# Rounding keys and queries in one pass, with the score factor in the minimum: an attention and mixing kernel on one core

## The chip, the cores and the metric

The kernel runs on one core of one Trainium2 chip. The metric is device time in microseconds (us) of one execution; the kernel before took 984.07 us (median of 3 runs, 982.93 to 987.56). The engines are named as the profile names them: PE is TensorE's matmul, PEld its weight load, DVE is VectorE, ACT is ScalarE, POOL is GpSimd, SP is SyncE, which here only issues transfers.

## What is computed

Three stages follow each other: a causal attention with a decay, a Fourier mixing with a feed-forward block, and a second mixing with weights of its own. The change touches the attention alone (4 batches of 8 heads, 576 positions, 64 columns a head):

```python
scores = scale * np.matmul(q, k.transpose(0, 1, 3, 2))     # scale = 1/8
cum = np.cumsum(np.log(np.clip(f, 0.0001, 1.0)), axis=-1)
decay = cum[:, :, :, None] - cum[:, :, None, :]
scores = np.where(causal, -1000000000.0, scores + decay)
scores = scores - np.max(scores, axis=-1, keepdims=True)
attn = np.exp(scores)
attn = attn / (np.sum(attn, axis=-1, keepdims=True) + 1e-09)
out = np.matmul(attn, v)
```

## The kernel before

`phase1` walks over 32 heads, in 16 pairs. The matmuls of the scores take a rounded type, so each of q and k is cut into a rounded upper part and a lower part (value minus upper part), and the products upper times upper, lower times upper and upper times lower are summed. The rows of one head's operands are laid out for two matmuls:

- `hi` (128 x 2 x 576): plane 1 is the query, plane 0 the key. Both stand twice in `raw`, in rows 0 to 63 and again in rows 64 to 127. Rows 64 to 127 of plane 1 are overwritten with the query's lower part. L232 multiplies plane 1 by plane 0.
- `q2` (66 x 576, one buffer for even heads and one for odd ones): a second copy of the rounded query in rows 0 to 63 and ones in rows 64 and 65. `kl` (66 x 2 x 576, one for a pair): the key's lower part in rows 0 to 63, the running sum of the decay, in an upper and a lower part, in rows 64 and 65. L233 multiplies `q2` by `kl` into the same bank.

`prep_units` makes these for a head, from a `raw` of 128 x 2 x 576 that `load_head` (L191) brings from memory over SP's queue; there are two `raw` buffers, so the load for one head waits until the last reader of the head two before it is done. Per head: ScalarE rounds the query (L200); GpSimd takes the query's difference (L201); ScalarE rounds the key times -0.125 (L206; in every fourth head GpSimd does it, L204); GpSimd copies the query into `q2` (L210); VectorE takes the key's lower part (L211, again with the factor -0.125). For head 0 VectorE and ScalarE do all of it.

`score_units` then runs L232 and L233 for five blocks of query rows, into three rotating PSUM banks `pa`. VectorE empties each bank with one instruction that adds the mask, keeps the result in `P` and writes the row's minimum (L241; the scores are negated, so the minimum stands for the maximum). ScalarE takes exp of the minimum minus `P` (L246). After every second head VectorE turns the row sums into reciprocals (L248, L249) and GpSimd spreads them (L252). `turn_units` transposes `P` on TensorE (L271) and copies it out (L275 on ScalarE, L277 on VectorE); `av_units` multiplies by v (L306); `evac_pair` scales the outcome on VectorE (L322, L328), sends three rows through SP's queue (L331 to L338) and forms a sum and a difference on GpSimd (L341 `E`, L343 `O`). `fft_units` does the Fourier step of the batch before in between (L370 to L440: VectorE folds, ScalarE rounds, TensorE multiplies, `u` is formed on VectorE or GpSimd).

The loop pulls these generators in turn, a head's preparation one round ahead of its scores. What order the instructions stand in on each engine is then settled by a scheduler by priorities (scores 20, products with v 40) and by readiness as it reckons it; each engine runs its own list strictly in that order and waits at its head. From about 270 us on, the feed-forward and the last stage follow, which the change does not touch.

Of the kernel before, what the change touches and what calls it, by code (L numbers as in the profile page):

```python
# [13 lines left out]
ALU = mybir.AluOpType  # L14
# [41 lines left out]
class Net:  # L56
# [37 lines left out]
    def p1_open(self):  # L94
# [43 lines left out]
            nc.gpsimd.memset(z, 1.0)  # L138
        with tc.manual_schedule(engines={mybir.EngineType.DVE, mybir.EngineType.Activation}):
            nc.vector.memset(one, 1.0)  # L140
            nc.vector.memset(flag, 1.0)
            nc.vector.memset(flag[0:1], 0.0)
            fs, cs, hs = ([x[:, g * S : g * S + S] for g in range(2)] for x in (f0, c0, h0))
            for g in range(2):
                nc.vector.tensor_scalar(fs[g], fs[g], 1e-4, 1.0, ALU.max, ALU.min)
                nc.scalar.activation(fs[g], fs[g], AF.Ln)
            nc.vector.tensor_tensor_scan(cs[0], one[64:66], fs[0], 0.0, ALU.mult, ALU.add)
            nc.vector.tensor_scalar(lf, lf, 1e-4, 1.0, ALU.max, ALU.min)
            nc.vector.tensor_scalar(hs[0], cs[0], -1.0, None, ALU.mult)
            nc.vector.scalar_tensor_tensor(kl[64:66, 0], f(hs[0]), flag, cs[0], ALU.mult, ALU.add)  # L150
            for _ in self.prep_units(0, pair, raws[0], heads[0]):
                pass
            nc.scalar.activation(lf, lf, AF.Ln)
            nc.scalar.activation(self.rz[0][:, 0, 0:1], self.mask[:, 448:449], AF.Exp, scale=-1.0)


        def rest():
            nc.vector.tensor_tensor_scan(cs[1], one[64:66], fs[1], 0.0, ALU.mult, ALU.add)
            yield
            nc.vector.tensor_scalar(hs[1], cs[1], -1.0, None, ALU.mult)  # L160
            nc.vector.scalar_tensor_tensor(kl[64:66, 1], f(hs[1]), flag, cs[1], ALU.mult, ALU.add)
            yield from self.prep_units(1, pair, raws[1], heads[1])
            nc.vector.tensor_tensor_scan(cum, one[0:32], lf, 0.0, ALU.mult, ALU.add)
            nc.gpsimd.tensor_scalar(ch[:, 0], cum, 1.0, 1.0, ALU.mult, ALU.mult)
            nc.gpsimd.tensor_tensor(ch[:, 1], cum, f(ch[:, 0]), ALU.subtract)
            nc.gpsimd.dma_start(self.scr, ch)
            yield
# [26 lines left out]
    def prep_units(self, n, pair, raw, hd):  # L194
        nc = self.nc
        g = n % 2
        kl, q2 = pair["kl"], self.q2[g]
        hi = self.w2.tile([128, 2, S], F32R, tag="hi", name="hi")
        hd["hi"] = hi
        nc.scalar.copy(hi[:, 1], raw[:, 1])  # L200
        (nc.vector if n == 0 or n % 4 in [] else nc.gpsimd).tensor_tensor(hi[64:128, 1], raw[64:128, 1], f(hi[64:128, 1]), ALU.subtract)  # L201
        yield
        if n > 1 and n % 4 in [0]:
            nc.gpsimd.tensor_scalar(hi[:, 0], raw[:, 0], -0.125, 1.0, ALU.mult, ALU.mult)  # L204
        else:
            nc.scalar.activation(hi[:, 0], raw[:, 0], AF.Copy, scale=-0.125)  # L206
        if n == 0:
            nc.scalar.copy(q2[0:64], raw[0:64, 1])
        else:
            nc.gpsimd.tensor_scalar(q2[0:64], raw[0:64, 1], 1.0, 1.0, ALU.mult, ALU.mult)  # L210
        nc.vector.scalar_tensor_tensor(  # L211
            kl[0:64, g], raw[0:64, 0], -0.125, f(hi[0:64, 0]), ALU.mult, ALU.subtract
        )
        yield

    def score_units(self, hd, g):
        nc = self.nc
# [6 lines left out]
        for i in (4, 3, 2, 1, 0):  # L224
# [5 lines left out]
            with self.tc.high_priority(20):  # L230
                for t, a, b in parts:
                    nc.tensor.matmul(t[:, 0 : b - a], hi[:, 1, q], hi[:, 0, a:b], start=True, stop=False)  # L232
                    nc.tensor.matmul(t[:, 0 : b - a], q2[:, q], kl[:, g, a:b], start=False, stop=True)  # L233
                p = P[:, POFF[i] : POFF[i] + n0 + 128]
                lowest, least = mn[:, i : i + 1], 3.0e38
                for t, a, b in parts:
                    if b - a < n0 + 128 and a == 0:
                        to = mn[:, 5:6]
                    else:
                        to = lowest  # L240
                    nc.vector.tensor_tensor_reduce(  # L241
                        out=p[:, a:b], in0=t[:, 0 : b - a], in1=self.mask[:, S - n0 - 128 + a : S - n0 - 128 + b],
                        scale=1.0, scalar=least, op0=ALU.add, op1=ALU.min, accum_out=to,
                    )
                    least = to
                nc.scalar.activation(p, p, AF.Exp, bias=lowest, scale=-1.0, accum_out=zs[:, g, i : i + 1])  # L246
# [842 lines left out]
def constants():  # L1089
# [30 lines left out]
    alt = np.where(np.arange(258) % 2 == 0, 1.0, -1.0).astype(np.float32)[None, :]  # L1120
    alt[0, 257] = 0.0
    alt = np.concatenate([alt, np.zeros((127, 258), np.float32)])
    mask = np.where(np.arange(128)[None, :] <= np.arange(128)[:, None], 0.0, 1e30).astype(np.float32)
    return dict(dft=dft, alt=alt, mask=mask, ident=np.eye(128, dtype=np.float32))


# [53 lines left out]
```

## Time and profile before

| | |
|---|---|
| median of 3 runs | 984.07 us |
| lowest, highest | 982.93, 987.56 us |
| the profiled execution | 982.28 us |
| its span (first to last instruction) | 980.5 us |
| TensorE, share of the span | 94% |
| VectorE | 66% |
| ScalarE | 44% |
| GpSimd | 32% |

The shares are means over three stages. After about 300 us, in the feed-forward and the mixing, TensorE is busy nearly all the time and GpSimd for long stretches not at all; in the attention, the first 270 us, all four engines carry work. A row of the trace gives the start of an instruction in us from the span's start, its length in us, the engine and line, the tiles written and read with their shapes, and in brackets how long the engine had been idle before it and who released it. A TensorE that counts as busy includes the tail of a matmul in its pipeline, so it can be fed somewhat more densely than its busy share says.

### The profile page before, as it was taken

What the parts mean: (1) busy time and instruction counts of PE and PEld (TensorE: products, weight loads), DVE (VectorE), ACT (ScalarE), POOL (GpSimd) and SP (SyncE); (2) the same over time, 40 slices, a digit from 0 to 9 for tenths busy, and PEclk for the clock granted to TensorE, in tenths of its full rate; (3) what the DMA queues carried; (4) which work ended last, traced back from release to release, by engine and by line L of the source; (5) the groups of instructions that cost most, each with busy time, mean ns of one, the idle gap of its engine ahead of it and who ended that gap; (6) DMA issues with size and microseconds to landing.
All of it is one profiled execution on the core that took longest, in us unless ns stands there. A gap on an engine that the chain in (4) does not pass through costs nothing.

```text
span 980.5 us, 15893 instructions
## 1 busy us (share of the span) xinstructions
PE 917.6 (94%) x5960; PEld 852.3 (87%) x5960; DVE 644.3 (66%) x1503; ACT 427.8 (44%) x1038; POOL 312.9 (32%) x376
## 2 busy tenths in 40 slices
PE   4889898988978898999999999999999999999998
PEld 3667676766757798999999999999999999999998
DVE  7868778668678787625665366545677765746554
ACT  5887767667463243312332122112335543535331
POOL 5756356366433243300000000000014744525330
PEclk9999999999998799999999999999999999999999
DMA  4743322313032112001222222232420000000001
GB/s 144 205 124 112 100 87 79 111 63 94 21 96 68 53 44 87 1 1 43 87 87 88 85 87 87 86 132 92 140 70 1 1 14 37 2 37 14 25 26 49
DMA packets 24336, 68.04 MB, mean 69 GB/s; under 512 B 3534, under 2 KB 6990, under 8 KB 24260
## 3 DMA queue, kind: packets, MB, share of 16 engines
q1 hardware_dynamic: 20420, 62.52, 19.8%
q0 software_dynamic: 3120, 3.33, 1.4%
q10 hardware_dynamic: 720, 1.18, 0.4%
q8 instruction: 47, 0.77, 0.3%
q14 instruction: 29, 0.24, 0.1%
HBM read 57.92 MB, written 9.07 MB: 68 GB/s over the span
## 4 chain that ended last, share of the span: by engine, by line
PE 59%; DVE 12%; ACT 2%; issue 2%; POOL 1%; DMA 1%; SPq 0%; ACTq 0%; DVEq 0%; POOLq 0%
PE pa L738 18%; PE pb L752 11%; PE po L752 8%; PE pb L959 5%; PE pa L970 4%; PE pa L923 4%; PE po L959 3%; PE pt L306 1%; DVE kra L930 1%; DVE kra L947 1%; DVE kra L933 1%; DVE a L556 1%; DMA raw<-in_wf 1%; PE pb L399 1%; DVE kra L932 1%
## 5 line engine op out<-in xcount | busy, mean ns | idle before, releaser
L738 PE MATMUL pa<-un,wf 128*128 128x384 f32 x1152 | 220.1, 339 | 4.7 <-ACT wf L563 2.4
L738 PEld LDWEIGHTS pa<-un,wf 128*128 128x128 f32 x1152 | 202.7, 190 | 6.7 <-ACT wf L563 2.6
L744 DVE SCALAR_TENSOR_TENSOR h<-pa,h 128x384 fp32r<-128x384 f32 x96 | 53.2, 556 | 145.2 <-ACT h L743 145.2
L752 PE MATMUL pb<-h,wf 128*128 128x384 f32 x660 | 135.2, 337 | 0.3 <-DVE u L760 0.3
L246 ACT ACTIVATE P<-P,mn 128x512 f32<-128x512 f32 (+4 forms) x160 | 95.8, 601 | 60.3 <-DVE mn L241 59.8
L752 PEld LDWEIGHTS pb<-h,wf 128*128 128x128 f32 x660 | 116.9, 189 | 0.9 <-DVE u L760 0.6
L743 ACT ACTIVATE h<-pa 128x384 fp32r<-128x384 f32 x96 | 46.7, 489 | 148.7 <-PE pa L738 148.6
L752 PE MATMUL po<-h,wf 128*128 128x384 f32 x492 | 104.2, 340 | 2.9 <-DVE h L744 2.0
L959 PE MATMUL pb<-wtk,z 128*128 128x288 f32 x513 | 97.0, 294 | 0.0
L241 DVE CUSTOM_DVE_ANT_0 P<-pa,mask 128x512 f32<-128x512 f32 (+4 forms) x160 | 77.7, 508 | 28.7 <-PE pa L233 21.6
L915 POOL COPY xd<-u 128x64 f32<-128x64 f32 x32 | 6.8, 254 | 272.5 <-DVE u L760 264.3
L752 PEld LDWEIGHTS po<-h,wf 128*128 128x128 f32 x492 | 87.5, 190 | 4.3 <-DVE h L744 2.3
L271 PE MATMUL pb<-ident,P 128*128 128x128 f32 x480 | 83.8, 283 | 8.0 <-ACT PT L275 3.8
L232 PE MATMUL pa<-hi 128*128 128x448 f32 (+2 forms) x192 | 69.1, 383 | 20.4 <-DVE hi L201 11.1
L949 POOL TENSOR_TENSOR z<-kra,z 128x256 fp32r<-128x256 f32 x72 | 53.8, 766 | 86.9 <-ACT z L948 86.9
L959 PEld LDWEIGHTS pb<-wtk,z 128*128 128x128 f32 x513 | 79.2, 188 | 0.0
L959 PE MATMUL po<-wtk,z 128*128 128x288 f32 x351 | 75.1, 295 | 1.1 <-POOL z L949 1.1
L306 PE MATMUL pt<-PT,v 128*64 128x256 f32 (+4 forms) x448 | 66.6, 381 | 8.7 <-DVE X L322 3.6
L271 PEld LDWEIGHTS pb<-ident,P 128*128 128x128 f32 x480 | 56.7, 143 | 19.4 <-ACT PT L275 6.8
L233 PE MATMUL pa<-kl,q 66*128 66x448 f32 (+2 forms) x192 | 63.2, 363 | 1.4 <-DVE kl L211 1.4
L923 PE MATMUL pa<-wf,xs 128*128 128x256 f32 x456 | 63.9, 289 | 0.0
L232 PEld LDWEIGHTS pa<-hi 128*128 128x128 f32 x192 | 38.0, 202 | 29.7 <-ACT hi L206 11.0
(201 smaller groups left out, 1706.9 us busy)
## 6 DMA issues: line engine op xcount, KB each, us to landing
raw<-in_qk SPq DMA_DIRECT2D x31, 576.0 KB, 3.9
raw<-in_wf SPq DMA_DIRECT2D x32, 512.0 KB, 4.1
raw<-in_wtk SPq DMA_DIRECT2D x18, 288.0 KB, 2.8
v<-in_vp SPq DMA_DIRECT2D x16, 320.0 KB, 3.3
out<-ob SPq DMA_DIRECT2D x12, 288.0 KB, 2.1
dft<-in_dft POOLq DMA_DIRECT2D x8, 346.0 KB, 6.3
raw<-in_wth SPq DMA_DIRECT2D x4, 512.0 KB, 4.0
st_wth<-raw SPq DMA_DIRECT2D x4, 512.0 KB
```

The lines of the kernel that those rows point to most:

```text
L232: nc.tensor.matmul(t[:, 0 : b - a], hi[:, 1, q], hi[:, 0, a:b], start=True, stop=False)
L233: nc.tensor.matmul(t[:, 0 : b - a], q2[:, q], kl[:, g, a:b], start=False, stop=True)
L241: nc.vector.tensor_tensor_reduce(out=p[:, a:b], in0=t[:, 0 : b - a], in1=self.mask[:, S - n0 - 128 + a : S - n0 - 128 + b], scale=1.0, sca ...
L246: nc.scalar.activation(p, p, AF.Exp, bias=lowest, scale=-1.0, accum_out=zs[:, g, i : i + 1])
L271: nc.tensor.transpose(ps[:, o : o + 128], src, self.ident)
L306: nc.tensor.matmul(T[64 * g : 64 * g + 64, 256 + a : 256 + hi_q], v[:, j, g, :], hd["PT"][:, place[j, a] : place[j, a] + hi_q - a], start= ...
L738: nc.tensor.matmul(ps[:, 0:CH], t[:, l, 128 * d : 128 * d + 128], un[r][:, d], start=n == 0, stop=n == 11)
L744: nc.vector.scalar_tensor_tensor(h[:, 1], ps[:, 0:CH], 0.0, f(h[:, 0]), ALU.max, ALU.subtract)
L752: nc.tensor.matmul(outs[d], t[:, l, 128 * d : 128 * d + 128], h[:, r], start=k % G == 0 and n == 0, stop=k % G == G - 1 and n == 2,)
L923: nc.tensor.matmul(th, xs[:, l, d], self.wth[d][:, r, 256 * hf : 256 * hf + 256], start=n == 0, stop=n == 11)
L949: nc.gpsimd.tensor_tensor(z[:, 1], t, f(z[:, 0]), ALU.subtract)
L959: nc.tensor.matmul(acc[k][th], z[:, l, 128 * k : 128 * k + 128], self.wtk[kt][:, r, 288 * th : 288 * th + 288], start=first and i == 0 and ...
```

## The change

The factor 1/8 leaves the preparation. The instruction that empties the score banks (L241 before, L238 after) multiplies by -0.125 where it multiplied by 1; the mask is negated to fit, and the running sums of the decay are multiplied by -8, for heads 0 and 1 in the two instructions that make them anyway (L149, L150 and L160, L161), for all others by one more GpSimd instruction, once in the program (L164 after). Keys and queries need now only be rounded: one ScalarE copy of 128 x 1152 does both (L206 after). The two lower parts are two GpSimd differences in a row (L210 after). The copy of the rounded query into `q2` is a transfer on SP's queue from `hi` (L207 after). Head 0 keeps its own form: three ScalarE copies and two VectorE differences.

```diff
--- before.py
+++ after.py
@@ -138,7 +138,7 @@
             nc.gpsimd.memset(z, 1.0)
         with tc.manual_schedule(engines={mybir.EngineType.DVE, mybir.EngineType.Activation}):
             nc.vector.memset(one, 1.0)
-            nc.vector.memset(flag, 1.0)
+            nc.vector.memset(flag, 8.0)
             nc.vector.memset(flag[0:1], 0.0)
             fs, cs, hs = ([x[:, g * S : g * S + S] for g in range(2)] for x in (f0, c0, h0))
             for g in range(2):
@@ -146,21 +146,22 @@
                 nc.scalar.activation(fs[g], fs[g], AF.Ln)
             nc.vector.tensor_tensor_scan(cs[0], one[64:66], fs[0], 0.0, ALU.mult, ALU.add)
             nc.vector.tensor_scalar(lf, lf, 1e-4, 1.0, ALU.max, ALU.min)
-            nc.vector.tensor_scalar(hs[0], cs[0], -1.0, None, ALU.mult)
-            nc.vector.scalar_tensor_tensor(kl[64:66, 0], f(hs[0]), flag, cs[0], ALU.mult, ALU.add)
+            nc.vector.tensor_scalar(hs[0], cs[0], flag, None, ALU.mult)
+            nc.vector.scalar_tensor_tensor(kl[64:66, 0], cs[0], -8.0, f(hs[0]), ALU.mult, ALU.add)
             for _ in self.prep_units(0, pair, raws[0], heads[0]):
                 pass
             nc.scalar.activation(lf, lf, AF.Ln)
-            nc.scalar.activation(self.rz[0][:, 0, 0:1], self.mask[:, 448:449], AF.Exp, scale=-1.0)
+            nc.scalar.activation(self.rz[0][:, 0, 0:1], self.mask[:, 448:449], AF.Exp)
 
 
         def rest():
             nc.vector.tensor_tensor_scan(cs[1], one[64:66], fs[1], 0.0, ALU.mult, ALU.add)
             yield
-            nc.vector.tensor_scalar(hs[1], cs[1], -1.0, None, ALU.mult)
-            nc.vector.scalar_tensor_tensor(kl[64:66, 1], f(hs[1]), flag, cs[1], ALU.mult, ALU.add)
+            nc.vector.tensor_scalar(hs[1], cs[1], flag, None, ALU.mult)
+            nc.vector.scalar_tensor_tensor(kl[64:66, 1], cs[1], -8.0, f(hs[1]), ALU.mult, ALU.add)
             yield from self.prep_units(1, pair, raws[1], heads[1])
             nc.vector.tensor_tensor_scan(cum, one[0:32], lf, 0.0, ALU.mult, ALU.add)
+            nc.gpsimd.tensor_scalar(cum, cum, -8.0, 1.0, ALU.mult, ALU.mult)
             nc.gpsimd.tensor_scalar(ch[:, 0], cum, 1.0, 1.0, ALU.mult, ALU.mult)
             nc.gpsimd.tensor_tensor(ch[:, 1], cum, f(ch[:, 0]), ALU.subtract)
             nc.gpsimd.dma_start(self.scr, ch)
@@ -197,21 +198,17 @@
         kl, q2 = pair["kl"], self.q2[g]
         hi = self.w2.tile([128, 2, S], F32R, tag="hi", name="hi")
         hd["hi"] = hi
-        nc.scalar.copy(hi[:, 1], raw[:, 1])
-        (nc.vector if n == 0 or n % 4 in [] else nc.gpsimd).tensor_tensor(hi[64:128, 1], raw[64:128, 1], f(hi[64:128, 1]), ALU.subtract)
-        yield
-        if n > 1 and n % 4 in [0]:
-            nc.gpsimd.tensor_scalar(hi[:, 0], raw[:, 0], -0.125, 1.0, ALU.mult, ALU.mult)
-        else:
-            nc.scalar.activation(hi[:, 0], raw[:, 0], AF.Copy, scale=-0.125)
         if n == 0:
+            nc.scalar.copy(hi[:, 1], raw[:, 1])
+            nc.scalar.copy(hi[:, 0], raw[:, 0])
             nc.scalar.copy(q2[0:64], raw[0:64, 1])
         else:
-            nc.gpsimd.tensor_scalar(q2[0:64], raw[0:64, 1], 1.0, 1.0, ALU.mult, ALU.mult)
-        nc.vector.scalar_tensor_tensor(
-            kl[0:64, g], raw[0:64, 0], -0.125, f(hi[0:64, 0]), ALU.mult, ALU.subtract
-        )
-        yield
+            nc.scalar.copy(hi, raw)
+            nc.sync.dma_start(f(q2[0:64]), f(hi[0:64, 1]))
+        yield
+        for rows, out, k in ((slice(64, 128), hi[64:128, 1], 1), (slice(0, 64), kl[0:64, g], 0)):
+            (nc.vector if n == 0 else nc.gpsimd).tensor_tensor(out, raw[rows, k], f(hi[rows, k]), ALU.subtract)
+            yield
 
     def score_units(self, hd, g):
         nc = self.nc
@@ -240,7 +237,7 @@
                         to = lowest
                     nc.vector.tensor_tensor_reduce(
                         out=p[:, a:b], in0=t[:, 0 : b - a], in1=self.mask[:, S - n0 - 128 + a : S - n0 - 128 + b],
-                        scale=1.0, scalar=least, op0=ALU.add, op1=ALU.min, accum_out=to,
+                        scale=-0.125, scalar=least, op0=ALU.add, op1=ALU.min, accum_out=to,
                     )
                     least = to
                 nc.scalar.activation(p, p, AF.Exp, bias=lowest, scale=-1.0, accum_out=zs[:, g, i : i + 1])
@@ -1120,7 +1117,7 @@
     alt = np.where(np.arange(258) % 2 == 0, 1.0, -1.0).astype(np.float32)[None, :]
     alt[0, 257] = 0.0
     alt = np.concatenate([alt, np.zeros((127, 258), np.float32)])
-    mask = np.where(np.arange(128)[None, :] <= np.arange(128)[:, None], 0.0, 1e30).astype(np.float32)
+    mask = np.where(np.arange(128)[None, :] <= np.arange(128)[:, None], 0.0, -1e30).astype(np.float32)
     return dict(dft=dft, alt=alt, mask=mask, ident=np.eye(128, dtype=np.float32))
```

How the lists of instructions change is shown at one place that the prediction speaks of, the second head of the eleventh pair, whose query L200 rounds at 159.22 us. TensorE's list there before; `hi` with `kl,q_100` are that head's, `q_99` the head's before it, `P` and `PT` are of earlier heads:

```order
L233 MATMUL pa<-kl,q_99 128x128
L271 MATMUL pb<-ident,P 128x128 x3
L232 MATMUL pa<-hi 128x448
L232 MATMUL pa<-hi 128x128
L271 MATMUL pb<-ident,P 128x128 x4
L306 MATMUL pt<-PT,v 64x320 x2
L306 MATMUL pt<-PT,v 64x192 x2
L306 MATMUL pt<-PT,v 64x64 x2
L232 MATMUL pa<-hi 128x512
L233 MATMUL pa<-kl,q_100 128x448
L233 MATMUL pa<-kl,q_100 128x128
```

And after:

```order
L230 MATMUL pa<-kl,q_99 128x128
L268 MATMUL pb<-ident,P 128x128 x5
L229 MATMUL pa<-hi 128x448
L230 MATMUL pa<-kl,q_100 128x448
L268 MATMUL pb<-ident,P 128x128
L303 MATMUL pt<-PT,v 64x320 x2
L303 MATMUL pt<-PT,v 64x192 x2
L303 MATMUL pt<-PT,v 64x64 x2
L229 MATMUL pa<-hi 128x128
L230 MATMUL pa<-kl,q_100 128x128
```

The head's first matmul with `kl` and `q2` stood behind six products with v and three blocks of L232; it stands now right behind its own L229, ahead of the products with v.

VectorE's list at the same place before (`ee`, `oo`, `el` belong to the Fourier step, `X` to the pair before; a minimum is two rows, the second without inputs):

```order
L241 ISA P,mn<-pa,mask 128x256
L241 ISA mn 128x1
L370 TENSOR_TENSOR ee<-E 128x2x287
L374 TENSOR_TENSOR oo<-O 128x2x287
L371 COPY ee<-E 128x2x2
L241 ISA P,mn<-pa,mask 128x128
L241 ISA mn 128x1
L211 SCALAR_TENSOR_TENSOR kl<-raw,hi 64x576
L377 TENSOR_TENSOR el<-ee,eh 128x580
L322 TENSOR_TENSOR X<-pt,X 128x576
L241 ISA P,mn<-pa,mask 128x448
```

And after:

```order
L367 TENSOR_TENSOR ee<-E 128x2x287
L371 TENSOR_TENSOR oo<-O 128x2x287
L368 COPY ee<-E 128x2x2
L238 ISA P,mn<-pa,mask 128x256
L238 ISA mn 128x1
L238 ISA P,mn<-pa,mask 128x128
L238 ISA mn 128x1
L376 TENSOR_TENSOR ol<-oo,oh 128x576
L319 TENSOR_TENSOR X<-pt,X 128x576
L374 TENSOR_TENSOR el<-ee,eh 128x580
L238 ISA P,mn<-pa,mask 128x448
```

The key's lower part is gone from the list; the head's first minimum (128x448) still stands behind the folds of the Fourier step, now behind two roundings of them in place of one.

GpSimd's list there before and, below it, after:

```order
L185 DMA kl<-scr 2x2x576
L201 TENSOR_TENSOR hi<-raw,hi 64x576
L210 TENSOR_SCALAR q_100<-raw 64x576
L252 TENSOR_SCALAR wide<-rz_98 128x640
L341 TENSOR_TENSOR E<-X,Y 128x576
L343 TENSOR_TENSOR O<-X,Y 128x576
```

```order
L186 DMA kl<-scr 2x2x576
L210 TENSOR_TENSOR hi<-raw,hi 64x576
L210 TENSOR_TENSOR kl<-raw,hi 64x576
L338 TENSOR_TENSOR E<-X,Y 128x576
L340 TENSOR_TENSOR O<-X,Y 128x576
L249 TENSOR_SCALAR wide<-rz_98 128x640
```

The second difference takes the place of the copy into `q2`, in front of `E` and `O`.

## Rows read from the trace of the kernel before

**Rows 1.** The page's first part: busy time of each engine, share, instructions.

```profile
span 980.5 us, 15893 instructions
...
PE 917.6 (94%) x5960; PEld 852.3 (87%) x5960; DVE 644.3 (66%) x1503; ACT 427.8 (44%) x1038; POOL 312.9 (32%) x376
```

**Rows 2.** The view of stretches: length, engines' busy us (instructions), clock, transfers.

```profile
30.00:90.00 60.00, 54.38 (x386) 41.49 (x385) 44.66 (x144) 48.40 (x140) 37.32 (x42) 1.00 0.57 165
90.00:270.00 180.00, 164.76 (x1112) 127.55 (x1109) 131.94 (x376) 120.40 (x340) 95.43 (x107) 0.96 0.25 78
270.00:300.00 30.00, 21.87 (x137) 16.34 (x137) 24.23 (x51) 17.96 (x40) 13.34 (x13) 0.89 0.32 106
```

**Rows 3.** The chain that ended last, 220 to 285 us: start, length, engine, line.

```profile
220.97 0.47 DVE P L241
221.80 1.13 DVE kl L211
...
257.45 0.67 DVE kl L211
...
258.99 1.95 POOL u L440
...
284.60 0.59 ACT Y L287
```

**Rows 4.** Groups by line and shape: busy us, mean ns of one, idle before.

```profile
L201 POOL TENSOR_TENSOR hi<-raw,hi 64x576 fp32r<-64x576 f32 x31 | 45.8, 1478 | 31.2 <-ACT hi L200 29.6 <-ACT P L246 0.6
...
L211 DVE SCALAR_TENSOR_TENSOR kl<-raw,hi 64x576 fp32r<-64x576 f32 x32 | 31.8, 994 | 1.9 <-ACT hi L206 1.3 <-POOL hi L204 0.4
...
L210 POOL TENSOR_SCALAR q<-raw 64x576 fp32r<-64x576 f32 x31 | 22.5, 725 | 14.1 <-PE pa L233 10.9 <-DMA raw<-in_qk 1.2 <-PE pb L271 1.1
...
L200 ACT CAST hi<-raw 128x576 fp32r<-128x576 f32 x32 | 21.5, 672 | 1.1 <-issue 0.5 <-PE pa L233 0.4
...
L206 ACT ACTIVATE hi<-raw 128x576 fp32r<-128x576 f32 x25 | 17.1, 686 | 0.0
...
L901 ACT CAST xs<-u 128x512 fp32r<-128x512 f32 x16 | 9.8, 615 | 15.1 <-PE pa L923 13.6 <-PE po L752 1.5
...
L204 POOL TENSOR_SCALAR hi<-raw 128x576 fp32r<-128x576 f32 x7 | 5.3, 751 | 3.0 <-PE pa L232 3.0
```

**Rows 5.** The same view, TensorE alone, 12 to 285 us: a head's first matmuls.

```profile
L233 PE MATMUL pa<-kl,q 66*128 66x448 f32 x32 | 14.5, 453 | 1.4 <-DVE kl L211 1.4
...
L232 PE MATMUL pa<-hi 128*128 128x448 f32 x31 | 14.2, 459 | 2.7 <-POOL hi L201 2.7
```

**Rows 6.** Timeline: one head's preparation, from its first rounding to its L233.

```profile
159.22 0.66 ACT L200 CAST hi<-raw 128x576 fp32r<-128x576 f32 x1
...
160.47 1.40 POOL L201 TENSOR_TENSOR hi<-raw,hi 64x576 fp32r<-64x576 f32 x1
...
162.49 0.67 ACT L206 ACTIVATE hi<-raw 128x576 fp32r<-128x576 f32 x1
...
168.02 0.74 DVE L211 SCALAR_TENSOR_TENSOR kl<-raw,hi 64x576 fp32r<-64x576 f32 x1
...
169.68 1.08 PE L233 MATMUL pa<-kl,q 66*128 66x448 f32 x3
```

**Rows 7.** Timeline at 232 us, and the view of L248 (min/median/max ns).

```profile
231.85 3.03 DVE L248 TENSOR_SCALAR rz<-zs 128x10 f32<-128x10 f32 x1
...
232.07 1.41 POOL L341 TENSOR_TENSOR E<-X,Y 128x576 f32<-128x576 f32 x1
...
233.45 1.39 POOL L343 TENSOR_TENSOR O<-X,Y 128x576 f32<-128x576 f32 x1
...
L248 DVE TENSOR_SCALAR rz<-zs x16: 157/632/3030, 25.5 to 276.3; 128x10 f32<-128x10 f32 x16
```

**Rows 8.** Transfers of 144 KB: issues, KB each, median us to landing.

```profile
out<-ob SPq DMA_DIRECT2D x4, 144.0 KB, 3.4
...
scr<-ch POOLq DMA_DIRECT2D x1, 144.0 KB, 2.3
```

## The prediction

> **What bounds the kernel now.** I read the busy shares first: TensorE 94%, and no other engine above 66% [rows 1]. That is a mean over stages, so the next view is the one of stretches. In the attention, from 30 to 270 us, TensorE is busy 54.38 + 164.76 = 219.1 of 240 us (91%), VectorE 176.6 (74%), ScalarE 168.8 (70%), GpSimd 132.8 (55%) [rows 2]. No engine is full: four lists, each run in its own order, wait for one another, and 21 us of TensorE stand idle. From 270 to 300 us TensorE falls to 21.87 of 30 while VectorE has 24.23; the last Fourier step is in hand there. After that the stages are untouched, so what the attention gains or loses moves the end by the same amount. The chain of waits is followed back only to 221 us, but its last 64 us of attention are a fair sample: from 220.97 to 284.60 + 0.59 us [rows 3] it changes engine every microsecond or two, and the key's lower part on VectorE (L211) is on it twice, with 1.13 and 0.67 us.
>
> Last I followed single heads. In the head of [rows 6] the query is rounded at 159.22, its difference is ready at 160.47 + 1.40 = 161.87, but the key is rounded only at 162.49 (its instruction stands further back in ScalarE's list) and its lower part is made at 168.02, since VectorE has the Fourier folds in front of it. The first L233 starts at 169.68, 0.92 us after that lower part ends. The preparation that took four short instructions was spread over 9.5 us.
>
> **The change, part by part.** All terms are set against the profiled execution, 982.28 us (span 980.5 and 1.8 around it); the median is 984.07, 1.8 above it, and I carry the sum over to the median.
>
> *VectorE loses L211.* 31 of 32 go, at 0.994 us: 30.8 us [rows 4], most of it in the attention, where VectorE's share falls from 74% towards 62%. How much is on the path? All of it would be 30.8, none of it 0. The chain has 1.13 + 0.67 = 1.80 us of it in 64.2 us [rows 3]; over the 245 us from 25 to 270 that is 1.80 x 245 / 64.2 = 6.9 us. I take -6.9, since that row is the only one that measures it on the path.
>
> *The minimum's factor.* It is the same instruction with another constant; nothing hides a cost, and I put none. The negated mask, the decay's factor for heads 0 and 1 and the extra GpSimd pass over 32 x 576 (one instruction, about the 0.73 of L210 [rows 4], once, before the third head) are 0 to 0.7 us; I take 0.
>
> *ScalarE.* One copy of 1152 columns replaces two of 576. From 615 ns for 512 columns and 672 for 576 [rows 4] a column costs 0.89 ns, so I estimate 672 + 576 x 0.89 = 1185 ns. 24 heads paid 672 + 686 = 1358, seven paid 672 (GpSimd did their key): 24 x 0.173 less 7 x 0.513 is 0.6 us saved. Zero on the path.
>
> *GpSimd gains.* 31 second differences at 1.478 come, 31 query copies at 0.725 and seven key roundings at 0.751 go [rows 4]: 45.8 - 22.5 - 5.3 = +18.0 us, from 55% to about 62% of the stretch. Where the copy stood, a difference stands now that is 0.75 us longer, and `E` and `O` wait behind it (GpSimd's list in the section on the change). Eight such pairs of sums make at most 6.0 us; nothing if GpSimd would have been idle before them. With 45% of its time idle I take +1.5.
>
> *VectorE held up by GpSimd.* L248 works on 10 columns and takes 0.157 us at best, yet one takes 3.03: it starts at 231.85 and ends at 234.88, when `E` (1.41) and `O` (1.39) have run back to back [rows 7]. 16 of them with a median of 0.632 lose some 16 x (0.632 - 0.157) = 7.6 us at least. Two differences back to back make such runs more frequent. In proportion to GpSimd's added busy time (18.0 / 132.8 = 14%) that is +1.0 us of VectorE; if each of the 16 met one more difference, 16 x 1.41 = 22.6. On the path at the share found above (6.9 / 30.8 = 22%) these are 0.2 and 5.0; I take +1.0. The Trainium skill (SBUF — State Buffer, section "SBUF: two separate sides") has VectorE and GpSimd take one pair of ports as an exclusive lock, held for a whole instruction, the other side blocking fully. By that rule a VectorE instruction waits for one GpSimd instruction, 1.4 us, and this term would be near 0.2; the 3.03 us of the row agree with the blocking but outlast one instruction, which speaks against so low a price and against putting two differences in a row.
>
> *The start of the scores.* TensorE stood idle 1.4 us for L211 and 2.7 for L201 in front of a head's first matmuls [rows 5], 4.1 in all. With one rounding, both differences follow at once: for the head of [rows 6] 159.22 + 1.19, then from 160.47 two differences of 1.40 end at 163.3, five microseconds before L211 did. The gain is between 0 and 4.1; TensorE's new list puts the first L230 right behind its L229, which uses the earlier time, while VectorE's puts the head's first minimum behind the same folds as before, which doesn't. I take -3.0.
>
> *The transfer.* 144 KB land 2.3 to 3.4 us after their issue [rows 8]; the two differences end 2 x 1.41 = 2.8 us after the rounding. So the copy comes between 0.5 us before and 0.6 us after the other operand. Only where a head's first L230 is short of time does that count; odd heads, whose rounding stands late in the list, are 15: 0 to 9 us, and I take +1.0. On SP's queue the transfer waits for the rounding and for the last L230 of the head two before; behind it is queued the load of a later `raw`, which has to wait for GpSimd's second difference of the same or an earlier head anyway, and the row transfers of `evac_pair`, which wait up to the time of one rounding.
>
> Sum: -6.9 + 1.5 + 1.0 - 3.0 + 1.0 = -6.4 us: 975.9 for the profiled execution, **977.7** for the median.
>
> **The rivals.**
> *A, the full gain.* If VectorE really paces the attention, what leaves it leaves the time: half to two thirds of 30.8, plus the 4.1 of [rows 5], -19 to -25 us, 959 to 965. For it: VectorE is second in [rows 2], and ScalarE and TensorE both wait for its minima. Against it: only 1.80 of 64 us on the chain.
> *B, nothing.* TensorE is 91% busy, its work is unchanged, and the order of the lists, not the load of VectorE, makes the waits; the head of [rows 6] has its minimum behind the same folds as before. What VectorE gives back comes as idle time: -2 to +3, 982 to 987.
> *C, slower.* The runs of GpSimd. 16 L248 and some 20 instructions of the Fourier step with two operands in SBUF can be held up. If each of the 36 waits for one difference more, VectorE gets 36 x 1.41 = 51 us and loses 30.8: +20. At the 22% on the path that is +4.4; if `E` and `O` come late as well (6.0), +10: 988 to 994. It decides from the point where more than 30.8 / 1.41 = 22 of the 36 are met. For it: the 3.03 us of [rows 7]. Against it: the 32 exposures of L211 itself, 0.994 against 0.74 when free [rows 4, 6], are gone.
> *D, the change doesn't prepare earlier.* Where SP's queue stands at another transfer, `q2` lands late and TensorE waits at L230 ahead of the products with v. At 1 us in each of 15 odd heads the gain is used up and 8 us more: 992. It shares C's sign; I give it little, as the loads of v in front of it were issued early.
>
> **How the numbers follow.** Forecast (-2.5 to -13) 0.44, A 0.13, B 0.26, C 0.12, D 0.05. A measurement of this kernel tells about 0.5% (4.9 us) from no change. Below 979.2 lie A and most of the forecast (0.38): faster 0.51. Within: the forecast's upper edge (0.06), B and a little of C and D: 0.34. Slower: 0.15. The range goes from 965 (the weak end of A) to 988 (the beginning of C).
>
> **What would show it.** In the trace after: no VectorE L211 but in head 0; VectorE near 150 of 240 us from 30 to 270, TensorE's busy time unchanged in a shorter stretch; the 128x1152 copies near 1.19 us; 62 GpSimd differences near 1.45; L230 (448 columns) seldom released by the transfer. I am wrong if L246 waits for the minima as long as before (B), if L248's median rises well above 0.632 and `O` releases ScalarE late (C), or if L230 waits for SP's transfer (D).

## The result, and the profile after

The changed kernel took 994.58 us (median of 7 runs, 989.44 to 996.21), the kernel before 985.14 us beside it (7 runs, 982.34 to 987.56). The ratio is 1.0090, 95% interval 1.0064 to 1.0115: slower by 0.9%, where 977.7 was forecast. The profiled execution took 994.51 us, its span is 992.7.

The page's first part, which answers [rows 1]:

```profile
span 992.7 us, 15898 instructions
...
PE 923.1 (93%) x5960; PEld 855.3 (86%) x5960; DVE 619.6 (62%) x1472; ACT 429.0 (43%) x1014; POOL 329.4 (33%) x370
```

The span grew by 12.2 us. TensorE has the same 5960 matmuls and is busy 5.5 us longer (923.1 against 917.6); the other 6.7 us it stood idle. Not all of that is the change: the medians lie 9.4 us apart, and `f1_factor_same_list` below, which runs the four engines' lists of before in 1.0015 of the time, has 921.8 us of busy TensorE in its trace. The view of stretches, with the columns of [rows 2], says where:

```profile
30.00:90.00 60.00, 51.42 (x338) 38.69 (x338) 32.10 (x121) 45.88 (x125) 37.39 (x36) 0.94 0.60 169
90.00:270.00 180.00, 161.98 (x1086) 125.21 (x1083) 111.23 (x340) 119.44 (x319) 101.02 (x97) 0.93 0.32 98
270.00:300.00 30.00, 25.03 (x184) 18.37 (x183) 21.17 (x55) 17.91 (x44) 16.56 (x19) 1.00 0.27 82
```

From 30 to 270 us VectorE has 143.3 us instead of 176.6, as the change intends; but in the same time TensorE does 1424 of its matmul records instead of 1498, at 0.94 and 0.93 of its clock instead of 1.00 and 0.96. The last exponential of a head is a good mark to compare kernels by. In the two traces it ends at (us):

| head | 3 | 4 | 5 | 9 | 11 | 12 | 21 | 31 | end |
|---|---|---|---|---|---|---|---|---|---|
| before | 37.8 | 44.5 | 51.5 | 79.3 | 93.4 | 101.0 | 178.0 | 274.8 | 980.5 |
| after, later by | 0.4 | 2.6 | 4.4 | 6.7 | 6.3 | 10.4 | 11.5 | 11.4 | 12.2 |

Nearly all of the loss is there by head 12. Groups of instructions, 12 to 290 us, which answer [rows 4] and the view of L248 in [rows 7]:

```profile
L206 ACT CAST hi<-raw 128x1152 fp32r<-128x1152 f32 x30 | 34.7, 1155 | 5.3 <-issue 4.8 <-PE pa L229 0.4
...
L210 POOL TENSOR_TENSOR kl<-raw,hi 64x576 fp32r<-64x576 f32 x31 | 44.7, 1440 | 2.1
L210 POOL TENSOR_TENSOR hi<-raw,hi 64x576 fp32r<-64x576 f32 x31 | 44.5, 1435 | 56.8 <-ACT hi L206 37.0 <-issue 17.7 <-POOL wide L249 1.1
...
L245 DVE TENSOR_SCALAR rz<-zs 128x10 f32<-128x10 f32 x16 | 9.1, 570 | 3.9 <-ACT P L243 3.6
```

The parts cost what was forecast (1155 ns for the copy, 1440 and 1435 for the differences). The waits are new. Of the view of waits, 12 to 290 us (engine, tile and line, what it waited for: us in total, times, longest), first the kernel before:

```profile
ACT P L246 <- DVE mn L241: 59.8, 40, 7.6
...
DVE X L322 <- PE pt L306: 7.8, 4, 3.6
...
ACT X L287 <- POOL O L343: 3.0, 3, 1.3
...
PE pt L306 <- ACT X L288: 2.7, 3, 1.7
...
PE pb L271 <- ACT X L287: 1.9, 1, 1.9
```

and the changed kernel:

```profile
ACT P L243 <- DVE mn L238: 48.2, 27, 7.4
...
DVE X L319 <- PE pt L303: 11.9, 3, 5.7
ACT X L284 <- POOL O L340: 10.9, 5, 2.9
...
PE pt L303 <- ACT X L285: 5.4, 2, 2.9
DVE ee L367 <- POOL E L338: 5.4, 3, 2.3
...
PE pb L268 <- ACT X L284: 5.1, 2, 3.0
...
PE pa L230 <- DMA q<-hi: 4.2, 2, 3.4
```

ScalarE waits less for the minima, as it should with VectorE relieved. What is late instead is GpSimd's `O`: ScalarE's copy into `X` waits for it 10.9 us instead of 3.0, and TensorE waits for the copies into `X` 5.4 and 5.1 us instead of 2.7 and 1.9. New as well are TensorE's 4.2 us for the query transfer `q` and 2.1 us for the key's difference (`kl`, L210). The timeline around 72 us shows one place where `O` is late:

```profile
71.46 1.42 POOL L210 TENSOR_TENSOR kl<-raw,hi 64x576 fp32r<-64x576 f32 x1
...
72.84 1.41 POOL L338 TENSOR_TENSOR E<-X,Y 128x576 f32<-128x576 f32 x1
...
74.21 1.39 POOL L340 TENSOR_TENSOR O<-X,Y 128x576 f32<-128x576 f32 x1
...
75.64 0.59 ACT L284 COPY X<-pb 128x512 f32<-128x512 f32 x1 [2.90 <-POOL O L340]
...
76.39 1.70 PE L303 MATMUL pt<-PT,v 128*64 128x320 f32 x12 [2.56 <-ACT X L285]
...
78.23 0.76 DVE L319 TENSOR_TENSOR X<-pt,X 128x576 f32<-128x576 f32 x1 [5.74 <-PE pt L303]
```

The second difference, `E` and `O` run back to back; the next `X` can be copied only when `O` has read the old one, and the products with v stand in TensorE's list behind that. In the stretches of 4 us there TensorE is busy 1.38 of 4, GpSimd 4.00 of 4, and TensorE's granted clock is 0.62 in the next:

```profile
72.00:76.00 4.00, 1.38 (x9) 0.83 (x7) 0.49 (x4) 1.10 (x5) 4.00 (x4) 1.00 0.45 139
76.00:80.00 4.00, 3.61 (x19) 2.43 (x20) 0.76 (x1) 3.17 (x9) 1.43 (x2) 0.62 0.20 50
```

At 103 us, in head 12, the folds of the Fourier step on VectorE take part as well:

```profile
103.35 1.41 POOL L338 TENSOR_TENSOR E<-X,Y 128x576 f32<-128x576 f32 x1
...
104.73 1.39 POOL L340 TENSOR_TENSOR O<-X,Y 128x576 f32<-128x576 f32 x1
104.80 1.94 DVE L367 TENSOR_TENSOR ee<-E 128x574 f32<-128x574 f32 x1 [1.36 <-POOL E L338]
106.15 0.59 ACT L284 COPY X<-pb 128x512 f32<-128x512 f32 x1 [2.52 <-POOL O L340]
106.19 1.80 POOL L210 TENSOR_TENSOR hi<-raw,hi 64x576 fp32r<-64x576 f32 x1
...
106.65 1.96 DVE L371 TENSOR_TENSOR oo<-O 128x574 f32<-128x574 f32 x1
...
108.07 1.79 POOL L210 TENSOR_TENSOR kl<-raw,hi 64x576 fp32r<-64x576 f32 x1
108.53 1.36 DVE L368 COPY ee<-E 128x4 f32<-128x4 f32 x1
```

`ee` starts 0.07 us behind `O` and ends 0.6 us after it; from there the two engines take turns, and a copy of four columns lasts 1.36 us. The stretches (same columns) show TensorE idle, then at 0.50 of its clock, the lower of its two levels (1.2 of 2.4 GHz), for some 8 us:

```profile
104.00:108.00 4.00, 1.89 (x13) 1.00 (x13) 3.21 (x2) 0.70 (x2) 3.92 (x3) 0.96 0.30 96
108.00:112.00 4.00, 1.08 (x9) 0.60 (x5) 3.92 (x6) 2.74 (x8) 1.79 (x1) 0.50 0.24 47
112.00:116.00 4.00, 3.98 (x18) 1.96 (x18) 1.49 (x7) 2.13 (x6) 0.00 (x0) 0.50 0.46 184
```

### The profile page after: what moved, and what is told of

The parts are those of the page before. It is cut to its first block, busy times and chain, and to the rows that moved or that the text cites. A ratio compares the mean times of both kernels' runs of the same rounds, so it can differ in the third digit from the quotient of the medians.

```text
span 992.7 us, 15898 instructions
## 1 busy us (share of the span) xinstructions
PE 923.1 (93%) x5960; PEld 855.3 (86%) x5960; DVE 619.6 (62%) x1472; ACT 429.0 (43%) x1014; POOL 329.4 (33%) x370
## 4 chain that ended last, share of the span: by engine, by line
PE 62%; DVE 9%; ACT 2%; issue 2%; POOL 1%; DMA 1%; SPq 0%; ACTq 0%; DVEq 0%; POOLq 0%
PE pa L735 18%; PE pb L749 11%; PE po L749 8%; PE pb L956 5%; PE pa L920 4%; PE pa L967 4%; PE po L956 3%; PE pt L303 2%; DMA raw<-in_wf 1%; DVE kra L927 1%; DVE kra L944 1%; DVE a L553 1%; PE pa L916 1%; PE pb L396 1%; DVE kra L930 1%
## 5 line engine op out<-in xcount | busy, mean ns | idle before, releaser
L243 ACT ACTIVATE P<-P,mn 128x256 f32<-128x256 f32 (+4 forms) x160 | 95.7, 600 | 52.1 <-DVE mn L238 48.2
L238 DVE CUSTOM_DVE_ANT_0 P<-pa,mask 128x448 f32<-128x448 f32 (+4 forms) x160 | 77.6, 509 | 35.0 <-PE pa L230 24.2
L268 PE MATMUL pb<-ident,P 128*128 128x128 f32 x480 | 85.8, 288 | 14.0 <-ACT PT L272 6.1
L229 PE MATMUL pa<-hi 128*128 128x448 f32 (+2 forms) x192 | 70.2, 384 | 17.5 <-ACT hi L206 10.5
L303 PE MATMUL pt<-PT,v 128*64 128x320 f32 (+4 forms) x448 | 67.6, 391 | 7.1 <-ACT X L285 5.4
L230 PE MATMUL pa<-kl,q 66*128 66x448 f32 (+2 forms) x192 | 64.2, 363 | 6.5 <-DMA q<-hi 4.2
L210 POOL TENSOR_TENSOR hi<-raw,hi 64x576 fp32r<-64x576 f32 x31 | 44.5, 1435 | 56.8 <-ACT hi L206 37.0
```

The source lines that it names most:

```text
L238: nc.vector.tensor_tensor_reduce(out=p[:, a:b], in0=t[:, 0 : b - a], in1=self.mask[:, S - n0 - 128 + a : S - n0 - 128 + b], scale=-0.125, ...
L268: nc.tensor.transpose(ps[:, o : o + 128], src, self.ident)
L303: nc.tensor.matmul(T[64 * g : 64 * g + 64, 256 + a : 256 + hi_q], v[:, j, g, :], hd["PT"][:, place[j, a] : place[j, a] + hi_q - a], start= ...
```

## The experiments

Three theories. **L**: the second difference makes longer runs of GpSimd work; `E` and `O`, and those who wait for them, come late. **T**: the query transfer lands late. **O**: any edit makes the scheduler put the instructions in another order, and the order of before is simply a good one. All ratios below are to the kernel before on the same chip, with 95% intervals.

### Undoing parts of the change

`e1_key_on_dve`: the keys' lower part back on VectorE.

```diff
-            (nc.vector if n == 0 else nc.gpsimd).tensor_tensor(out, raw[rows, k], ...)
+            (nc.vector if n == 0 or k == 0 else nc.gpsimd).tensor_tensor(out, raw[rows, k], ...)
```

> The changed kernel with the keys' lower part (its second GpSimd difference, 31 of about 1.44 us) given back to VectorE; the query's difference stays on GpSimd, the transfer stays. Theory L (runs of two-input GpSimd work: the second difference stands ahead of E and O, ScalarE's X copies and VectorE's folds wait, TensorE idles and its granted clock falls): 983 to 989 us, ScalarE X waiting for O some 3 us instead of 10.9, the mean of the four ee folds back from 1.64 to about 1.32 us. Theory T (the late transfer at head 4 is what costs): 992 to 995, since the transfer is as it was. Theory O (any move of the list costs some us by itself): anything, with waits at other places than these.

`e2_q2_by_copy`: the query copy by ScalarE; `e3_both_undone`: both edits.

```diff
-            nc.sync.dma_start(f(q2[0:64]), f(hi[0:64, 1]))
+            nc.scalar.copy(q2[0:64], raw[0:64, 1])
```

> The changed kernel with the query copy as a ScalarE copy from the raw tile instead of the transfer on SP. Theory T: the 3.4 us wait of TensorE at head 4 is gone and the end is 3 to 6 us earlier, 988 to 991; then the scores of head 4 start about 3 us sooner. Theory L: the GpSimd runs are as they were, 992 to 996, and ScalarE has 31 copies of 64x576 more (each estimated at about 0.6 us, half of the 1155 ns of the 128x1152 copy).

> Both edits together: the keys' lower part on VectorE and the query copy on ScalarE. What is left of the change is the factor in the minimum, the one-pass rounding, and the query's difference. Theory L: as the run with the key's part on VectorE, within 3 us (983 to 989). Theory T: as the run with the copy on ScalarE (988 to 991). If both cost: the two gains add, 980 to 986.

`e4_factor_only`: the preparation of before without the factor; minimum, mask and running sums as in the change.

> The kernel before with the score factor alone moved into the minimum: two rounding copies, the query copy on GpSimd, the keys' lower part as a plain difference on VectorE. L and T both expect the time of the kernel before within 3 us (982 to 988), the mean of a minimum unchanged. If the factor itself costs (a slower minimum, or the order that the list takes), it is 990 or more.

Measured: e1 992.0 us, 1.0097 (1.0069 to 1.0126); e2 994.5, 1.0108 (1.0080 to 1.0136); e3 997.6, 1.0143 (1.0115 to 1.0170); e4 994.9, 1.0122 (1.0095 to 1.0149). None comes back, not even the one with the factor alone: neither L nor T as put. The marks tell why these four do not separate them. In e1, e3 and e4 the last exponential of head 2 is already 5.4, 4.8 and 7.3 us late, in the changed kernel 0.2 early. GpSimd's timeline of `e1_key_on_dve` there:

```profile
24.95 0.73 POOL L178 DMA_DIRECT2D dft<-in_dft  x1
25.77 0.71 POOL L249 TENSOR_SCALAR wide<-rz 128x640 f32<-128x640 f32 x1
26.44 0.77 POOL L178 DMA_DIRECT2D dft<-in_dft  x1
28.84 1.14 POOL L186 DMA_DIRECT2D kl<-scr  x2 [1.64 <-DMA scr<-ch]
```

The load of the decay's rows for heads 2 and 3 is issued at 28.84, after a wait of 1.64 us for the transfer `scr<-ch` that it reads from; in the changed kernel at 21.53. That transfer was issued at 24.39 instead of 18.91 and landed after 4.2 us instead of 2.3, with a matrix load issued right behind it. Undoing a part had moved the lists elsewhere. So the order had to be held, or be varied by itself.

### The order by itself, and the factor by itself

`l0_list_only`: the kernel before, with the two operands of the instructions for the decay's rows exchanged (`flag` is -1 to fit).

```diff
-            nc.vector.tensor_scalar(hs[1], cs[1], -1.0, None, ALU.mult)
-            nc.vector.scalar_tensor_tensor(kl[64:66, 1], f(hs[1]), flag, cs[1], ALU.mult, ALU.add)
+            nc.vector.tensor_scalar(hs[1], cs[1], flag, None, ALU.mult)
+            nc.vector.scalar_tensor_tensor(kl[64:66, 1], cs[1], 1.0, f(hs[1]), ALU.mult, ALU.add)
```

> The kernel before with the same work; only the operands of the two 2x576 instructions that make the gates' rows of heads 0 and 1 stand the other way round (sum first, rounded part second). The scheduler then puts the instructions of heads 0 to 13 in another order on every engine; from head 13 on the order is that of before. Theory O (the order that the scheduler happens to give is what costs): 990 to 997 us, all of the loss by the exponentials of head 13. Theories L and T (GpSimd runs, transfer; no part of the change is in this kernel): 982 to 987, as before.

`b1_before_prio21`: `high_priority(20)` becomes `high_priority(21)` in the kernel before.

> The kernel before with the same work and one number of the scheduler changed: the score matmuls' priority 20 is 21. The order moves in small pieces through all heads. Theory O: slower than before by 3 to 12 us, 988 to 997, if the order of before is a good draw; theories L and T: 982 to 987.

`f1_factor_same_list`: the factor in the minimum, -8 in the two constant rows of `q2` in place of the factor on the decay.

```diff
-            nc.gpsimd.memset(f(z[64:66]), 1.0)
+            nc.gpsimd.memset(f(z[64:66]), -8.0)
...
-                        scale=1.0, scalar=least, op0=ALU.add, op1=ALU.min, accum_out=to,
+                        scale=-0.125, scalar=least, op0=ALU.add, op1=ALU.min, accum_out=to,
```

> The kernel before with the factor alone moved into the minimum, written so that TensorE's order is that of before instruction for instruction: keys unscaled, the two rows of ones in the queries' copy hold -8 in place of the factor on the gates, no GpSimd multiply in the opening. Theory O: 982 to 987 us, the time of before, where the run with the factor alone and another order took 994.9. If the factor itself costs: 990 or more.

`a1_rows_as_before`: the changed kernel with that same way of the factor, so with the opening of before.

> The changed kernel with the opening of before (gates' rows and their order of operands as before, the factor -8 in the queries' two constant rows, no GpSimd multiply). All the parts of the change that touch every head stay. Theory L: 992 to 996, since the GpSimd runs and their waits are the same. Theory O: another order and so another time, anywhere from 978 to 997; the forecast's 977.7 holds only if the order is as good as that of before.

Measured: l0 989.6 us, 1.0065 (1.0040 to 1.0091); b1 983.6, 0.9998 (0.9980 to 1.0016); f1 984.9, 1.0015 (0.9993 to 1.0036); a1 996.7, 1.0135 (1.0101 to 1.0168). The same work in another order costs 0.65% in one draw and nothing in another, so O is real, up to that size. The factor costs nothing when TensorE's order is kept: its heads run within 0.5 us of those of before up to head 20. The 2.9 us that it loses at head 21 are neither work nor order, for all four lists are those of before: from 164 to 168 us TensorE is busy 2.12 us before and 2.11 in f1, and in the next two stretches of 4 us its granted clock is 0.69 and 1.00 before, 0.50 and 0.50 in f1. So a single trace carries a few us of chance. And the changed kernel stays over 1% slower with the opening of before: its loss is not an accident of the opening.

### The parts added one at a time, opening of before

`p1_one_pass` is f1 with one 128 x 1152 copy in place of the two roundings (GpSimd's seven included); `p2_key_on_pool` is p1 with the keys' lower part on GpSimd; `p3_transfer` is p1 with the query copy as a transfer; a1, above, has both.

> The factor alone with the order of before (984.9 us measured) plus the one-pass rounding: one ScalarE copy of 128x1152 a head in place of two passes; the query copy is on GpSimd and the keys' lower part on VectorE, as in before. Theories L and T: 982 to 988, since neither the second GpSimd difference nor the transfer is in it. Theory O or a cost of the one pass itself (the queries' rounding, of which the scores' first matmuls wait, comes when the whole copy is done): 990 or more.

> As the run with factor and one-pass rounding, plus the keys' lower part on GpSimd, which then has three operations of 64x576 a head (two differences and the query copy); no transfer. Theory L: slower than the run without this step by 5 to 10 us, 990 to 996. Theory T: the same as that run within 3 us.

> As the run with factor and one-pass rounding, plus the query copy as a transfer on SP; the keys' lower part stays on VectorE. Theory T: slower than the run without this step by 5 to 12 us, with waits of TensorE for the transfer in heads 3 to 9. Theory L: the same as that run within 3 us.

| | query copy on GpSimd | query copy by transfer |
|---|---|---|
| keys' lower part on VectorE | p1 1.0037 (1.0015 to 1.0059), 988.3 us | p3 1.0060 (1.0038 to 1.0082), 990.1 us |
| keys' lower part on GpSimd | p2 1.0132 (1.0104 to 1.0159), 998.4 us | a1 1.0135 (1.0101 to 1.0168), 996.7 us |

The step to GpSimd costs 0.95% in one column and 0.75% in the other, the transfer 0.2% and nothing. In p2 against p1 `O` is late as in the changed kernel, and TensorE waits 7.7 us for the key's difference (1.2 in p1, where VectorE makes it); one line of p1, two of p2:

```profile
ACT X L283 <- POOL O L339: 5.9, 3, 2.5
```

```profile
ACT X L283 <- POOL O L339: 11.1, 4, 3.5
...
PE pa L229 <- POOL kl L209: 7.7, 5, 4.2
```

`t2_loads_in_opening` is a1 with the matrix loads issued before head 0 (`if n < 0: for j in range(8): self.load_dft(j, None)`; VectorE's copy that held each load back goes too), since in a1 transfers are late among those loads, as this piece of its timeline shows (issue 46.43, use 53.60):

```profile
46.43 0.47 SPq L206 DMA_DIRECT2D q<-hi  x1
...
49.72 0.74 POOL L177 DMA_DIRECT2D dft<-in_dft  x1
...
53.60 0.50 PE L229 MATMUL pa<-kl,q 66*128 66x448 f32 x2 [3.44 <-DMA q<-hi]
```

> The changed kernel with the opening of before, and its eight 346 KB loads of the transform's matrix issued in the opening instead of in heads 2 to 5. In the run without this move head 3's exponentials ended at 42.7 and head 9's at 96.0 us (53.3 us between, 41.5 in before), and TensorE waited 6.1 us there for three late query transfers. Theory T (the query transfer, 7 us from issue to use among these loads, is what loses heads 3 to 9): heads 3 to 9 take 42 to 46 us, no wait for the transfer over 1 us there, the end 985 to 991 less what the opening loses. Theory L (GpSimd runs) and theory O (order): heads 3 to 9 take 48 us or more.

Measured: 999.7 us, 1.0139 (1.0110 to 1.0168). Heads 3 to 9 take 50.0 us instead of 53.3 (before 41.5). From head 3 to head 6 it is 21.9 instead of 25.8 (before 21.2), so there the late transfer was the cost; but heads 7 to 9 still lose, and the opening loses 7 us at head 3. T is a real cost of a few us in one place, and not the cause.

### Second draws of the order

Priority 21 for 20 in p1, p2 and a1.

> The run with factor and one-pass rounding (988.3 us measured), same work, the scheduler's priority 21 for 20: a second draw of the order. If the order alone makes the differences (theory O): anywhere from 982 to 998. If the work does (theory L): within 4 us of the first draw, 984 to 992.

> The run with the keys' lower part on GpSimd as well (998.4 us measured), same work, priority 21 for 20: a second draw. Theory L: it stays 6 us or more above the second draw of the kernel without that step, 993 or more. Theory O: no fixed distance to it, and 982 to 992 is as likely.

> The changed kernel with the opening of before (996.7 us measured), same work, priority 21 for 20: a second draw. Theory L: 991 to 1000. Theory O: anywhere from 980 to 1000.

Measured: p1 995.3 us, 1.0115 (1.0069 to 1.0162); p2 1007.3, 1.0245 (1.0212 to 1.0279); a1 1007.0, 1.0244 (1.0210 to 1.0278). This draw is worse for all three by 0.8 to 1.1%, which the kernel before did not show; O again. But the step from p1 to p2 is there again: 1.3%. It survives the change of order, but not by the same path: in this draw of p2 TensorE waits 10.3 us for the key's difference itself and never for `X`, and ScalarE waits 6.6 us for `O`.

### `E` and `O` away from GpSimd's queue

If the second difference hurts because `E` and `O` stand in the same queue, then it should stop hurting when they don't.

```diff
-        nc.gpsimd.tensor_tensor(E[:, k], X, Y, ALU.add)
+        nc.vector.tensor_tensor(E[:, k], X, Y, ALU.add)
         yield
-        nc.gpsimd.tensor_tensor(O[:, k], X, Y, ALU.subtract)
+        nc.vector.tensor_tensor(O[:, k], X, Y, ALU.subtract)
```

In p2:

> The run with the keys' lower part on GpSimd, and the sum E and the difference O of two heads' pairs (16 operations of 128x576, 1.4 us each) given to VectorE, which the change relieves. If what costs is that E and O stand behind the second difference on GpSimd (ScalarE's X waited 11.1 us for O, VectorE's folds 6.4 us for E): 986 to 992, the waits of X for O below 4 us. If the costs are elsewhere (TensorE's 7.7 us for the keys' lower part at the start of scores, the order): 994 to 1001.

in the changed kernel as it was given:

> The changed kernel exactly as it was given (994.6 us), with the pair sum E and difference O on VectorE. If the GpSimd queue in front of E and O is what the change loses: 982 to 989, the heads' end within 5 us of before (274.8 us), ScalarE's X waiting for O under 4 us where the changed kernel has 10.9. Theory O: 990 to 998.

and, as the control, in the kernel before:

> The control: the kernel before with E and O on VectorE, nothing else. If moving E and O off GpSimd is a gain only where GpSimd has the second difference: 983 to 992 (VectorE has 16 operations more, some 12 to 20 us of work beside TensorE's). If it is a gain for any kernel: 972 to 981, and then the recovery in the changed kernel says nothing of the change.

Measured: p2 goes from 1.0132 to 1.0063 (1.0036 to 1.0089), 989.1 us. The changed kernel goes from 1.0090 to **0.9958 (0.9936 to 0.9979), 981.8 us** against 985.75 for before beside it. The control stays at 1.0007 (0.9984 to 1.0030), 986.7 us. The edit gives back 0.7% and 1.3% where GpSimd has the second difference and nothing where it hasn't. In the changed kernel with it the waits and stretches are

```profile
PE pb L268 <- ACT X L284: 4.5, 4, 1.7
...
PE pt L303 <- ACT X L285: 3.7, 2, 2.0
...
ACT X L284 <- DVE O L340: 2.7, 3, 1.3
...
ACT X L285 <- DVE O L340: 2.5, 1, 2.5
...
DVE X L319 <- PE pt L303: 2.0, 1, 2.0
```

```profile
30.00:90.00 60.00, 54.73 (x364) 40.26 (x366) 36.92 (x129) 48.74 (x132) 35.88 (x35) 0.97 0.63 182
90.00:270.00 180.00, 166.60 (x1143) 129.36 (x1144) 122.46 (x373) 122.64 (x330) 96.82 (x98) 0.96 0.32 95
```

ScalarE waits 5.2 us for `O` instead of 10.9, VectorE 2.0 instead of 11.9 for the products behind it, TensorE's clock is back at 0.97 and 0.96, and the last exponential of head 31 stands at 272.6 us: 13.6 before that of the changed kernel, 2.2 before that of the kernel before. But more than `E` and `O` changed. The 5.2 us are above the 4 expected, and TensorE's waits for `X` fell only from 10.5 to 8.2 us, while those for the query transfer fell from 4.2 to 0.8 and those for the key's difference from 2.1 to nothing. In p2 the waits for `X` did not fall (6.1 to 6.7), those for the key's difference did (7.7 to 4.0). So the two runs show time coming back when `E` and `O` leave GpSimd's queue; through which of the waits, they do not show.

**What stays open.** Every edit redraws the order, and draws differ by up to 1.1%. That holds for the two runs with `E` and `O` on VectorE too: each is one draw, and 0.7% is within what draws differ by. In the given opening, e1 against the changed kernel and e3 against e2 show no cost of the second difference in the whole time (-0.1% and -0.35%). Of e1 the marks say why: from head 3 to head 31 it loses 4.7 us, the changed kernel 11.0; the rest it lost at head 2. For e3 against e2 (10.9 and 11.3 us) they don't. And whether the 0.4% by which the last version beats the kernel before is the change or a good draw was not tried with a second one.

## Why the prediction was wrong

- *L211 leaves VectorE, -6.9.* It left (143.3 of 240 us, "near 150" forecast), and ScalarE waits 11.6 us less for the minima (59.8 to 48.2). Whether this is worth anything is not shown: with `E` and `O` out of the way the kernel is 0.42% faster than before, about 4 us, and that is within what an order is worth.
- *The factor, 0.* Right: 1.0015 with the order kept.
- *ScalarE's one pass, 0 on the path.* The duration was right (1155 ns for 1185). p1 is 0.2% above f1, with intervals that overlap; TensorE waits 8.5 us for the query's difference there, 2.7 in f1.
- *`E` and `O` behind a longer operation, +1.5, at most 6.0.* **This step failed.** It counted 0.75 us for each of eight pairs and then took most of it away because GpSimd is idle 45% of the time. That share is a mean over 240 us. Where `E` and `O` stand GpSimd is busy 4.00 of 4 us, a whole difference of 1.4 us is in front of them, and what follows is not a delay of the same length: TensorE's list stops at the products with v, and TensorE comes back at a lower clock. TensorE's waits for `X` rose from 4.6 to 10.5 us. The two runs with `E` and `O` on VectorE give back 0.7 to 1.3%, 7 to 13 us, in which other waits and the draw have a share that is not known.
- *VectorE held up, +1.0.* The place is wrong, and what it costs on the path was not measured; in VectorE's own time it nearly cancels. L245 got shorter (mean 817 to 570 ns, 16 of them: -4.0 us). The three Fourier steps in the stretch got longer: mean 1512 to 1936 ns for `ee`, 1072 to 1494 for `oo`, 316 to 964 for the copy, together 3 x 1.494 = +4.5 us. The timeline at 103 us agrees with the rule of the Trainium skill (SBUF — State Buffer, section "SBUF: two separate sides") that, where VectorE's instruction reads two inputs from SBUF or runs in a mode that takes both port pairs, whichever of the two engines starts first holds the shared ports for its whole instruction: each waits for one instruction of the other there, and no more.
- *The start of the scores, -3.0.* **This step failed too:** wrong in sign. The two groups of [rows 5], 2.7 and 1.4 us of idle TensorE, are now 2.7 and 6.5: 4.2 for the transfer, 2.1 for the key's difference on GpSimd. So 5.1 us were added where 3.0 were to go, nearly as much as the waits for `X` added (5.9). Standing right behind its L229, L230 waits for its operand where the products with v used to fill the time; that is read from the lists and was not tried by itself.
- *The transfer, +1.0, 0 to 9.* Within the bounds, but not where I looked. The landing was taken from rows with little else on the queues (2.3 and 3.4 us); the median is 2.4 us, and one among the matrix loads takes 6.9.
- *TensorE's busy time, unchanged.* It is 5.5 us longer; how much of that is the change is not known, as f1 with the lists of before has 4.2 us more than before.
- *The rivals.* C comes nearest in time (988 to 994) and has half the mechanism: late `O`, yes; L248, no. It had 0.12; what was held against it was that L211's own delays are gone, and the late `E` and `O` were in it only as an "if". D's wait is there, 4.2 us for the transfer where D reckoned with 15, but p3 prices the transfer at 0.2%. That an edit redraws the order, and that this alone is worth up to 1.1% here, was not among the rivals at all.

## What to carry to other kernels

Work moved onto an engine with spare time is priced at the queue it joins: look which instructions with a waiting reader stand behind it in that engine's list, and at the engine's busy share in those microseconds, not over the stage. Where a scheduler makes the lists, run the old kernel once or twice with a neutral change of order first, and hold the order when pricing a part; otherwise parts and draws can't be told apart. When an offload loses, moving the waiting neighbour out of the way may be better than undoing it: here that turned 0.9% slower into 0.4% faster, in the one order tried.

## What the runs showed of the hardware

- TensorE's idle time can cost more than itself, and not the same each time. In the changed kernel it was busy 2.97 of the 8 us from 104 to 112, and from 108 to 116 it ran at 0.50 of its clock. After one and the same gap at 164 us the next two stretches of 4 us ran at 0.69 and 1.00 in the kernel before, at 0.50 and 0.50 in f1 with the same lists, and f1 lost 2.9 us there.
- One program's time moves with the clock that it is granted: in 102 runs beside the experiments the kernel before took 978.24 to 990.23 us, the four fastest at a mean clock of 0.988 or 0.989, the four slowest at 0.974 to 0.979. That spread, 12 us, is wider than the loss of the change, so two single runs could not settle it.
- VectorE and GpSimd can block each other in turn: GpSimd's difference, 1.40 us when free, took 1.80, and a VectorE copy of four columns took 1.36 (mean of three 0.96; 0.32 in the kernel before).
- The 144 KB transfer from `hi` to `q2` took 2.4 us from issue to landing at the median, and 6.9 us where loads kept the transfers' share at 1.12 and 1.09 (32 to 36 and 36 to 40 us).
